# A gated linear attention feeding four experts: the state of two heads kept in 96 columns, their last features side by side

## The chip, the cores and the metric

The kernel runs on one core of a Trainium2 chip. The metric is the device time of one execution in microseconds (us). Engines are named as in the profile: PE is TensorE's matmuls and PEld its weight loads, DVE is VectorE, ACT is ScalarE, POOL is GpSimd, and SP is the queue that issues most DMAs.

## The reference: what is computed

```python
# q, k, v, alpha: (4 batches, 8 heads, 768 steps, 48 features)
for t in range(S):
    state = alpha[:, :, t, :, None] * state + einsum('bhd,bhe->bhde', k[:, :, t], v[:, :, t])
    y[:, :, t] = einsum('bhd,bhde->bhe', q[:, :, t], state)
x = y.transpose(0, 2, 1, 3).reshape(3072, 384)          # rows: batch and step; columns: head, feature
p = domain_probs / (domain_probs.sum(-1, keepdims=True) + 1e-9)
for e in range(4):                                        # w1: 384 x 1024, w2: 1024 x 384
    h = maximum(x @ w1[e], 0)
    out += p[:, e:e + 1] * (h @ w2[e])
```

Everything is float32. Each head carries a 48 x 48 state through 768 steps. The result of the eight heads, 384 columns, goes through four two-layer experts whose outputs are mixed by `p`.

## The kernel before

**Units.** The 768 steps are cut into 6 blocks of 128 (`cb`), and a unit is one block of one batch, all 8 heads: 24 units, in `attention(u)`. Heads are taken in pairs. A pair has 128 rows: 64 for each head, of which 48 hold features and 16 are zero. Within a unit, the scores between the 128 steps are built in seven levels (`copy_q`, `next_q`, `next_k`, `products`, `take`), and end in `lat`, a 128 x 128 matrix for each head. `QT` holds the decayed queries of the pairs, turned so that features are rows. `KT` holds the decayed keys.

**What a unit does with values and state.** `rv` holds v for the unit, 128 steps by 8 heads by 64 columns (`values`, two buffers). For the even head of a pair the 48 features lie in columns 0 to 47, with zeros behind. For the odd head the first 32 features lie in columns 0 to 31 and the last 16 (`TAIL`) in columns 48 to 63, with zeros between. `load` therefore moves v in three DMAs (L166 to L168) on SP's queue, one for the even heads and two for the odd ones. `sts[b]` is the state of batch b: 128 rows (features of the key, both heads of the pair) by 4 pairs by 2 heads by 64 columns (features of the value, laid out as in `rv`). Rows of one head against columns of the other stay zero, as they were set at the start.

**The read-out, L405 to L420.** `yps` receives the result turned, features in rows: 384 rows as 3 chunks of 128, each made of four strips of 32 rows. A turn is four matmuls, one for each strip. Each has 32 weight columns and 128 moving columns. Chunks 0 and 1 hold the first 32 features of the heads, one head to a strip. Chunk 2 holds the last 16 features of all heads, and a strip holds those of one pair: 16 of the even head, 16 of the odd head. Its strip is summed over two turns, one for each head, where the zeros beside each head's tail keep the other head's rows unchanged. A turn over the past multiplies the state with `QT`. A turn over the unit's own steps multiplies `rv` with `lat`. Units of the first block (`cb == 0`, 4 of the 24) have no past.

**The state update, L430 to L446,** is done for all blocks but the last: the keys are turned on PE and copied by ACT to `KB`; four matmuls, one for each pair, write keys with values into `sps` (L437, 128 weight columns, 128 moving columns). Then DVE, for each head of the pair, copies the sum into the state (block 0, L443) or multiplies the state with the decay of the block (L445) and adds the new sum (L446).

**Order of the work.** Nothing here is reordered by a scheduler: the program runs under a manual schedule, and each engine takes its instructions in the order in which the Python code emits them. The experts run in groups of up to four units. `up` makes hidden activations (L488, L496), `down` the outputs (L572, L576), `add_up` adds them to the accumulators on DVE (L603). `attention` is a generator with 17 beats, and `deal` gives each beat a due time from fixed estimates in `cost`. `advance`, called inside `up` and `down`, runs those beats that have come due. So the attention of the next units is dealt out between the experts' matmuls. In most groups the experts' products are made in three terms, and ACT and DVE prepare the parts between `up` and `down` (L503, L505, L528, L530, L538). At the start, matmuls on zeros (`fill`, L681, reading the last batch's state) keep PE running.

**DMAs.** Inputs, weights and most split weights come through SP's queue; `load(u + 2, "v")` is issued at the end of a unit for the unit two later. POOL clears `sts`, `values` and other tiles at the start (L659 to L667).

Of the kernel before, what the change touches and what calls it, by code (L numbers as in the profile page):

```python
# [10 lines left out]
F32 = mybir.dt.float32  # L11
# [9 lines left out]
def kernel(  # L21
# [37 lines left out]
    nc = tc.nc  # L59

    B, H, S, D = q.shape
    E, DM, F = moe_w1.shape
    P = 128
    NCB = S // P
    NP = H // 2
    HD = 64
    QUAD = 32
    TAIL = D - QUAD
# [13 lines left out]
    j = np.arange(P)[:, None] % HALF  # L82
    n = np.arange(QUAD)[None, :]
# [4 lines left out]
    const = ctx.enter_context(tc.tile_pool(name="const", bufs=1))  # L88
# [4 lines left out]
    ps = ctx.enter_context(tc.tile_pool(name="ps", bufs=2, space=bass.MemoryType.PSUM))  # L93
# [8 lines left out]

    near = const.tile([P, H, HALF], F32, name="near")
    lat = const.tile([P, H, P], F32, name="lat")
    sts = [const.tile([P, NP, 2, HD], F32, name=f"st{b}") for b in range(B)]

# [17 lines left out]
    def raw(u, nm):  # L126
        return values[u % 2] if nm == "v" else apart[nm] if u == 1 else early[nm]
# [26 lines left out]
    def load(u, names):  # L154
        if u >= len(units):
            return
        cb, b = units[u]
        for nm in names:
            src = srcs[nm][b, :, cb * P:(cb + 1) * P, :].rearrange("h s d -> s h d")
            if nm != "v":  # L160
                nc.sync.dma_start(out=raw(u, nm)[:, :, :D], in_=src)
                continue

            pairs = raw(u, nm).rearrange("p (a i) d -> p a i d", i=2)
            src = src.rearrange("p (a i) d -> p a i d", i=2)
            nc.sync.dma_start(out=pairs[:, :, 0, :D], in_=src[:, :, 0])  # L166
            nc.sync.dma_start(out=pairs[:, :, 1, :QUAD], in_=src[:, :, 1, :QUAD])
            nc.sync.dma_start(out=pairs[:, :, 1, D:], in_=src[:, :, 1, QUAD:])  # L168

# [86 lines left out]
    def turned(src):  # L258
        tp = ps.tile([P, NP, P], F32, name="tp", tag="w")
        for p in range(NP):  # L260
            nc.tensor.transpose(tp[:, p, :], src(p), ident)  # L261
        return tp

    def attention(u):
        cb, b = units[u]
        ra, rk, rq, rv = (raw(u, nm) for nm in ("a", "k", "q", "v"))
# [5 lines left out]
        nc.scalar.copy(out=AT, in_=turned(pair(ra)))  # L272
        after = u + 2 if u == 0 else u + 1 if u > 1 else len(units)
        load(after, "a")
        yield
        KT = keys()
# [3 lines left out]
        nc.vector.tensor_mul(own, rq[:, :, :D], rk[:, :, :D])  # L280
        nc.vector.reduce_sum(out=dot, in_=own, axis=AX.X)
        load(after, "k")
        yield
        nc.vector.tensor_mul(QT, turned(pair(rq)), AT)  # L284
        load(after, "q")
        yield

        decs = [AT]  # L290
# [91 lines left out]
        for r in range(NP // 2):  # L382
            for s in range(2):
                nc.tensor.matmul(far[HALF * s:HALF * (s + 1), r],
                                 lhsT=KTs[6][:, 2 * r + s, :HALF], rhs=qbs[6][:, 2 * r + s],
                                 start=True, stop=True)
# [8 lines left out]
        for s in range(2):  # L395
            rows = slice(HALF * s, HALF * (s + 1))
            nc.scalar.copy(out=parts[:HALF, :, s, :, HALF:], in_=far[rows])
        yield
        for s in range(2):
            rows = slice(HALF * s, HALF * (s + 1))  # L400
# [2 lines left out]
        yield  # L403

        st = sts[b]  # L405
        yps = ps.tile([P, KC, P], F32, name="yps", tag="w")
        for c in range(KC):

            if c < 2:
                turns = [[(j, 2 * c + j // 2, j % 2, slice(0, QUAD)) for j in range(4)]]  # L410
            else:
                turns = [[(p, p, i, slice(QUAD, HD)) for p in range(NP)] for i in range(2)]
            terms = [(t, past) for past in ((True, False) if cb > 0 else (False,)) for t in turns]
            for n, (turn, past) in enumerate(terms):
                for j, p, i, cols in turn:
                    nc.tensor.matmul(  # L416
                        yps[QUAD * j:QUAD * (j + 1), c, :],
                        lhsT=st[:, p, i, cols] if past else rv[:, 2 * p + i, cols],
                        rhs=QT[:, p, :] if past else lat[:, 2 * p + i, :],
                        start=(n == 0), stop=(n == len(terms) - 1))  # L420
        gi, slot = place[cb, b]
        if slot == 0:
            if gi == 0:
# [7 lines left out]
        if cb < NCB - 1:  # L431
            KB = AT
            nc.scalar.copy(out=KB, in_=turned(lambda p: KT[:, p, :]))
            yield
            sps = ps.tile([P, NP, 2, HD], F32, name="sps", tag="w")
            for p in range(NP):
                nc.tensor.matmul(sps[:, p], lhsT=KB[:, p, :], rhs=rv[:, 2 * p:2 * p + 2, :],  # L437
                                 start=True, stop=True)
            for i in range(2):
                rows = slice(HD * i, HD * (i + 1))  # L440
                old, add = st[rows, :, i, :], sps[rows, :, i, :]
                if cb == 0:
                    nc.vector.tensor_copy(out=old, in_=add)  # L443
                else:
                    nc.vector.tensor_mul(old, old, decs[-1][rows].broadcast_to([HD, NP, HD]))  # L445
                    nc.vector.tensor_add(old, old, add)  # L446

        load(u + 2, "v")
# [170 lines left out]
    def deal():  # L619

        wanted = [0.0]
        ends = [0.0, 0.0]
        events = []
        t = 0.0
        for gi in range(len(groups)):
            for e in range(E):
                part = 1 - 1 / len(groups[0]) if gi == e == 0 else 1
                t += cost(0, gi, e) * FCH * part  # L630
                if e == E - 1:
                    wanted.append(t)
                t += cost(1, gi, e) * len(groups[gi]) * part
        for gi in range(1, len(groups)):
            n = len(groups[gi])
            first = wanted[gi - 1] if gi > 1 else 0.0
            space = (wanted[gi] - MARGIN - first) / (n if gi > 1 else (n + 1) / 2)
            if gi == 1:
                space /= 2
            for k in range(n):  # L640
                u = sum(map(len, groups[:gi])) + k
                end = wanted[gi] - MARGIN - (n - 1 - k) * space
                begin = max(end - 2 * space, ends[-2])
                ends.append(end)
                run = attention(u)
                events += [(begin + (end - begin) * (j + 1) / BEATS, u, run) for j in range(BEATS)]
        return sorted(events, key=lambda x: x[:2])
# [7 lines left out]
    with tc.manual_schedule():  # L655
# [23 lines left out]
        def fill(n):  # L679
            for _ in range(n):  # L680
                nc.tensor.matmul(idle, lhsT=zeros, rhs=zeros, start=True, stop=True)  # L681

        runs = [attention(u) for u in range(len(groups[0]))]
        fill(8)
        for u, n in ((0, 3), (0, 6), (0, 4), (0, 5), (0, 5), (0, 4), (0, 3), (1, 0), (0, 0), (0, 2),
# [18 lines left out]
        for gi, e in ((gi, e) for gi in range(len(groups)) for e in range(E)):  # L704
# [5 lines left out]
            turns = [range(k, k + each) for k in range(rest, len(groups[gi]), each)]  # L710
# [41 lines left out]
```

## Time and profile before

| | |
|---|---|
| median of 7 runs | 1103.61 us (1103.15 to 1103.99) |
| the profiled execution | 1103.98 us, of which its span is 1102.2 us |
| busy in the span | PE 97%, PEld 82%, DVE 68%, ACT 51%, POOL 3% |
| granted TensorE clock, mean | 0.992 of full speed |
| DMA | 273.68 MB, mean 248 GB/s |
| matmul records | 8532; two for each plain float32 matmul |

A line of the group view gives the source line, the engine, the operation, the tiles written and read, the shape, the number of instructions, then the busy time of the group, the mean duration of one in ns, and the idle time of the engine before them with what ended it. Durations of matmuls overlap, since they are pipelined: a record of 275 ns can be followed by the next after 110 ns. The chain of waits is the chain of work that ended last: it is followed back from the end through whatever released each step.

### The profile page before, as it was taken

The numbers are of one execution on the slowest core, as the hardware profiler recorded it, in microseconds if no ns is written. First come the engines' busy times: TensorE is split into PE (matmuls) and PEld (weight loads), VectorE is DVE, ScalarE is ACT, GpSimd is POOL, SyncE is SP. The second block draws the span as 40 slices with busy tenths as digits, with TensorE's granted clock in tenths as the row PEclk, the third lists the DMA queues.
The fourth block names the chain that finished last, engine by engine and source line by source line (L and its number), as shares of the span: only waits on it lengthen the run. The fifth ranks groups of instructions, "written<-read, shape, count | busy, mean of one in ns | idle before, by whom it ended". The sixth has DMA issues, their size and how long they took to land.

```text
span 1102.2 us, 21700 instructions
## 1 busy us (share of the span) xinstructions
PE 1069.2 (97%) x8532; PEld 898.3 (82%) x8532; DVE 752.1 (68%) x1625; ACT 562.1 (51%) x1191; POOL 35.4 (3%) x75
## 2 busy tenths in 40 slices
PE   8889899999999999998999999899999999999998
PEld 8767677676776889897898898798888898898876
DVE  5577777656558868768778778787786776657211
ACT  5786776575556554544545535455444354323321
POOL 2000000000000000000000000000000000000000
PEclk9999999999999999999999999899999999999999
DMA  8597689877696965955758658477478468545882
GB/s 122 157 321 237 198 288 376 289 272 274 206 317 215 405 235 176 349 199 198 304 168 296 263 148 328 154 262 305 161 274 305 155 271 341 216 199 247 297 318 87
DMA packets 166197, 273.68 MB, mean 248 GB/s; under 512 B 120624, under 2 KB 140976, under 8 KB 142032
## 3 DMA queue, kind: packets, MB, share of 16 engines
q1 hardware_dynamic: 156704, 230.06, 59.8%
q0 software_dynamic: 6016, 42.08, 9.6%
q8 instruction: 67, 1.10, 0.4%
q10 hardware_dynamic: 3376, 0.17, 0.3%
q14 instruction: 34, 0.28, 0.1%
HBM read 229.81 MB, written 42.47 MB: 247 GB/s over the span
## 4 chain that ended last, share of the span: by engine, by line
PE 76%; DVE 14%; ACT 7%; issue 3%; DMA 1%; SPq 0%; ACTq 0%; DVEq 0%
PE ops L572 19%; PE one L496 17%; PE ops L576 14%; PE two L496 8%; PE sc L329 5%; PE yps L416 4%; PE one L488 3%; DVE hT L530 3%; DVE t L505 2%; DVE hT L538 2%; PE tp L261 2%; ACT qb L303 2%; ACT hT L528 2%; DVE near L339 2%; PE sps L437 1%
## 5 line engine op out<-in xcount | busy, mean ns | idle before, releaser
L572 PE MATMUL ops<-w,hT 128*128 128x384 f32 x1536 | 290.8, 344 | 12.1 <-DVE acc L603 11.9
L572 PEld LDWEIGHTS ops<-w,hT 128*128 128x128 f32 x1536 | 269.9, 190 | 17.4 <-DVE acc L603 14.5
L496 PE MATMUL one<-xT,w 128*128 128x512 f32 (+1 forms) x1104 | 274.8, 385 | 0.9 <-DVE hT L508 0.8
L496 PEld LDWEIGHTS one<-xT,w 128*128 128x128 f32 x1104 | 194.9, 188 | 42.6 <-issue 3.2
L503 ACT ACTIVATE t<-one 128x512 f32<-128x512 f32 (+1 forms) x184 | 103.2, 561 | 159.2 <-PE one L496 158.7
L303 ACT COPY qb<-QT 64x256 f32<-64x256 f32 x336 | 136.5, 406 | 81.4 <-DVE QT L284 48.0
L576 PE MATMUL ops<-hT 128*128 128x384 f32 x512 | 176.3, 492 | 0.0
L496 PE MATMUL two<-xT,w 128*128 128x512 f32 (+1 forms) x552 | 148.4, 377 | 0.0
L576 PEld LDWEIGHTS ops<-hT 128*128 128x128 f32 x512 | 94.0, 191 | 56.0 <-issue 0.8
L528 ACT ACTIVATE hT<-t 128x512 fp32r<-128x512 f32 x128 | 80.9, 632 | 97.3 <-DVE t L505 96.2
L530 DVE SCALAR_TENSOR_TENSOR hT<-t,hT 128x512 fp32r<-128x512 f32 x128 | 88.7, 693 | 61.1 <-ACT hT L528 59.7
L496 PEld LDWEIGHTS two<-xT,w 128*128 128x128 f32 x552 | 100.4, 188 | 19.7
L603 DVE SCALAR_TENSOR_TENSOR acc<-ops,p_all,acc 128x384 f32<-128x384 f32 x88 | 54.2, 617 | 75.2 <-PE ops L576 43.5
L538 DVE SCALAR_TENSOR_TENSOR hT<-hT 128x256 fp32r<-128x256 f32 x256 | 100.9, 422 | 4.4
L505 DVE TENSOR_TENSOR t<-t,two 128x512 f32<-128x512 f32 x128 | 87.4, 683 | 20.7 <-PE two L496 12.4
L339 DVE COPY_PREDICATED near<-masks,sc 128x256 f32<-128x256 uint8 x144 | 77.1, 535 | 21.7 <-PE sc L329 18.7
L329 PEld LDWEIGHTS sc<-qb,KT 128*64 128x64 f32 x2304 | 73.9, 140 | 9.6 <-issue 7.6
L329 PE MATMUL sc<-qb,KT 128*64 128x64 f32 x2304 | 78.2, 225 | 0.3 <-ACT qb L303 0.3
L508 DVE TENSOR_TENSOR hT<-t,two 128x512 f32<-128x512 f32 (+1 forms) x56 | 32.1, 574 | 67.2 <-ACT t L503 58.1
L310 DVE TENSOR_TENSOR QT<-QT,dec 128x256 f32<-128x256 f32 x144 | 60.8, 422 | 24.9 <-ACT qb L303 24.3
L322 DVE TENSOR_TENSOR KT<-KT,dec 128x256 f32<-128x256 f32 x144 | 60.4, 419 | 1.7 <-PE tp L261 1.5
L321 ACT COPY KT<-KT 128x256 f32<-128x256 f32 x144 | 59.8, 415 | 3.1
(79 smaller groups left out, 929.4 us busy)
## 6 DMA issues: line engine op xcount, KB each, us to landing
w<-kept SPq DMA_DIRECT2D x156, 1152.0 KB
kept<-w POOLq DMA_DIRECT2D x32, 1152.0 KB, 7.5
hT<-in_moe_w_dram SPq DMA_DIRECT2D x48, 384.0 KB
w<-in_moe_w_dram SPq DMA_DIRECT2D x60, 128.0 KB
ra<-in_alpha_dram SPq DMA_DIRECT2D x23, 192.0 KB
rk<-in_k_dram SPq DMA_DIRECT2D x23, 192.0 KB
rq<-in_q_dram SPq DMA_DIRECT2D x23, 192.0 KB
out_dram<-acc POOLq DMA_DIRECT2D x22, 192.0 KB, 6.6
```

Source lines behind the costliest of these rows:

```text
L303: nc.scalar.copy(out=qb[rows, :, i, :].rearrange("p a (b r) -> p a b r", r=m), in_=qv[rows])
L310: nc.vector.tensor_mul(qv, qv, spread(dv[:, :, :, 0], m))
L329: nc.tensor.matmul(out[HALF * s:HALF * (s + 1), 2 * p:2 * p + 2, :], lhsT=KTs[li][:, p, HALF * s:HALF * (s + 1)], rhs=qbs[li][:, p, :, QUA ...
L339: nc.vector.copy_predicated(near.rearrange("p a (b two r) -> p a b two r", two=2, r=m)[:, :, :, 1, :], mk.unsqueeze(1).broadcast_to([P, H, ...
L496: nc.tensor.matmul(out, lhsT=w[:, part, kc], rhs=xTs[gi][:, part, kc, :n], start=(part == terms[0] and kc == 0), stop=(part == terms[-1] a ...
L503: nc.scalar.activation(out=t, in_=one, func=ACT.Copy, scale=FINE)
L505: nc.vector.tensor_add(t, t, two)
L528: nc.scalar.activation(out=top, in_=x, func=ACT.Relu, scale=TRIM)
L530: nc.vector.scalar_tensor_tensor(out=low, in0=x, scalar=0.0, in1=top.bitcast(F32), op0=ALU.max, op1=ALU.subtract)
L538: nc.vector.scalar_tensor_tensor(out=dif, in0=top.bitcast(F32), scalar=1 / 4096.0, in1=low.bitcast(F32), op0=ALU.mult, op1=ALU.subtract)
L572: nc.tensor.matmul(sums[i][part // 2], lhsT=h[:, part], rhs=w, start=(fc == 0 and part != 1), stop=(fc == FCH - 1 and part != 0))
L576: nc.tensor.matmul(sums[i][0], lhsT=h[:, 2].bitcast(F32), rhs=w, start=(fc == 0), stop=(fc == FCH - 1))
```

## The change

State and keys-with-values are 48 columns a head in place of 64, so 96 for a pair. For the odd head the last 16 features now come first, followed by the first 32: in the 96 columns of a pair the two heads' tails stand side by side, in columns 32 to 63. In `rv` the head's 64 columns stay, with the odd head's tail in columns 0 to 15 and its first 32 features in columns 16 to 47. For the past, chunk 2 is read from the state in one turn, since one slice of 32 columns holds both tails and rows of one head are zero against the other's columns. For the unit's own steps chunk 2 is still read in two turns, with the zeros of `rv` beside each tail.

```diff
-    sts = [const.tile([P, NP, 2, HD], F32, name=f"st{b}") for b in range(B)]
+    sts = [const.tile([P, NP, 2, D], F32, name=f"st{b}") for b in range(B)]
...
-            nc.sync.dma_start(out=pairs[:, :, 1, :QUAD], in_=src[:, :, 1, :QUAD])
-            nc.sync.dma_start(out=pairs[:, :, 1, D:], in_=src[:, :, 1, QUAD:])
+            nc.sync.dma_start(out=pairs[:, :, 1, :TAIL], in_=src[:, :, 1, QUAD:])
+            nc.sync.dma_start(out=pairs[:, :, 1, TAIL:D], in_=src[:, :, 1, :QUAD])
...
         st = sts[b]
+        flat_st = st.rearrange("p a i d -> p a (i d)")
+        flat_v = rv.rearrange("p (a i) d -> p a (i d)", i=2)
         yps = ps.tile([P, KC, P], F32, name="yps", tag="w")
         for c in range(KC):
             if c < 2:
-                turns = [[(j, 2 * c + j // 2, j % 2, slice(0, QUAD)) for j in range(4)]]
+                now = [[(2 * c + j // 2, j % 2, (0, HD + TAIL)[j % 2], 2 * QUAD * (j % 2))
+                        for j in range(4)]]
+                turns = ([(True, now[0])] if cb > 0 else []) + [(False, now[0])]
             else:
-                turns = [[(p, p, i, slice(QUAD, HD)) for p in range(NP)] for i in range(2)]
-            terms = [(t, past) for past in ((True, False) if cb > 0 else (False,)) for t in turns]
-            for n, (turn, past) in enumerate(terms):
-                for j, p, i, cols in turn:
+                turns = [(True, [(p, 0, 0, QUAD) for p in range(NP)])] if cb > 0 else []
+                turns += [(False, [(p, i, QUAD + TAIL * i, 0) for p in range(NP)]) for i in range(2)]
+            for n, (past, turn) in enumerate(turns):
+                for j, (p, i, in_v, in_st) in enumerate(turn):
                     nc.tensor.matmul(
                         yps[QUAD * j:QUAD * (j + 1), c, :],
-                        lhsT=st[:, p, i, cols] if past else rv[:, 2 * p + i, cols],
+                        lhsT=flat_st[:, p, in_st:in_st + QUAD] if past
+                        else flat_v[:, p, in_v:in_v + QUAD],
                         rhs=QT[:, p, :] if past else lat[:, 2 * p + i, :],
-                        start=(n == 0), stop=(n == len(terms) - 1))
+                        start=(n == 0), stop=(n == len(turns) - 1))
...
-            sps = ps.tile([P, NP, 2, HD], F32, name="sps", tag="w")
+            sps = ps.tile([P, NP, 2, D], F32, name="sps", tag="w")
             for p in range(NP):
-                nc.tensor.matmul(sps[:, p], lhsT=KB[:, p, :], rhs=rv[:, 2 * p:2 * p + 2, :],
+                nc.tensor.matmul(sps[:, p], lhsT=KB[:, p, :], rhs=rv[:, 2 * p:2 * p + 2, :D],
                                  start=True, stop=True)
...
-                    nc.vector.tensor_mul(old, old, decs[-1][rows].broadcast_to([HD, NP, HD]))
+                    nc.vector.tensor_mul(old, old, decs[-1][rows].broadcast_to([HD, NP, D]))
```

## The prediction

> **What bounds the kernel now.** I read busy time by engine first, then the chain of waits, then the list of who waited for whom (us in total, times, longest).
>
> ```profile
> PE 1069.2 (97%) x8532; PEld 898.3 (82%) x8532; DVE 752.1 (68%) x1625; ACT 562.1 (51%) x1191; POOL 35.4 (3%) x75
> PE 76%; DVE 14%; ACT 7%; issue 3%; DMA 1%; SPq 0%; ACTq 0%; DVEq 0%
> ```
>
> ```profile
> PE ops L572 <- DVE acc L603: 11.9, 7, 3.8
> ```
>
> PE is the bound: it is idle for 33 us in all, and three quarters of the chain lie on it. The last line is its longest wait, for DVE's accumulation, where experts and attention together have filled DVE. PE waits for no DMA in that list. So a PE instruction saved counts if the chain runs through its burst, and DVE work counts only where the chain runs on DVE. The chain in order of time (start, length, work) tells which:
>
> ```profile
> 488.20 1.93 PE yps L416 x64
> ...
> 490.15 0.03 ACT x_raw L428
> ...
> 501.68 0.34 DVE st L445
> ...
> 518.63 0.54 DVE acc L603
> ...
> 519.22 4.67 PE ops L572 x17
> ...
> 1027.98 2.59 PE one L488 x12
> 1030.58 10.32 PE ops L576 x32
> ```
>
> The read-out's burst stands on the chain in all 20 units that have a past, from 124.98 to 980.69 us. After the one shown the chain goes through ACT to DVE, over the state update, to the accumulation that PE waits for. It crosses a whole state update so four times, at 501, 593, 676 and 769 us. It crosses the burst of sps in 15 of 20 units. The last two lines serve as a ruler: plain float32 matmuls follow each other every 0.216 us with 256 moving columns (2.59 / 12) and every 0.3225 us with 384 (10.32 / 32). Durations come from the groups with shapes kept apart (busy us, mean ns of one, idle before), and from the timeline (start, length from first start to last end):
>
> ```profile
> L416 PEld LDWEIGHTS yps<-QT,st 128*32 128x32 f32 x640 | 17.1, 109 | 7.3 <-issue 6.5 <-ACT hT L528 0.7
> L437 PEld LDWEIGHTS sps<-rv,AT 128*128 128x128 f32 x160 | 20.7, 191 | 3.9 <-ACT AT L433 1.8
> L329 PEld LDWEIGHTS sc<-qb,KT 128*64 128x64 f32 x2304 | 73.9, 140 | 9.6 <-issue 7.6 <-PE tp L261 1.1 <-ACT qb L303 0.8
> L446 DVE TENSOR_TENSOR st<-st,sps 64x256 f32<-64x256 f32 x32 | 13.4, 419 | 6.9 <-PE sps L437 5.0
> L312 DVE TENSOR_TENSOR dec<-AT 128x256 f32<-128x256 f32 x24 | 10.1, 419 | 0.0
> L312 DVE TENSOR_TENSOR dec<-dec 128x128 f32<-128x128 f32 x24 | 6.8, 285 | 0.0
> ```
>
> ```profile
> 489.03 0.62 PE L416 MATMUL yps<-QT,st 128*32 128x128 f32 x16
> 489.47 0.62 PE L416 MATMUL yps<-lat,rv 128*32 128x128 f32 x16
> 498.83 1.05 PE L437 MATMUL sps<-rv,AT 128*128 128x128 f32 x8
> ```
>
> **The change part by part.** The lists of instructions of the two kernels, engine by engine, are the same in order but for what follows.
>
> *The turn removed.* In chunk 2 the past takes one turn in place of two: 4 matmuls, 8 records, less in each of 20 units. Two turns over the past, 16 records, start at 489.03 and the next two at 489.47, so a turn takes 0.22 us: its four strips run beside each other, and its two records a strip follow each other after 109 ns. All 20 bursts are on the chain: 20 x 0.219 = 4.4 us. Its price is known; what could hide it is a second path nearly as long, which is a rival below. Waits of the burst for `lat` (7.7 us, 5 times) come at or before the other turns and stay.
>
> *Keys with values in 96 columns.* Four matmuls, 8 records, in 20 units, with the same 128 weight columns and 96 moving columns in place of 128. The records now follow each other after (1.05 - 0.276) / 7 = 0.111 us, 0.276 being the mean length of one in its group. No row has 96 columns, so I bound it. If the stream of columns set the pace, the ruler's (0.3225 - 0.216) / 128 = 0.83 ns a column gives 0.216 - 160 x 0.00083 = 0.083 us, which saves 8 x 0.028 = 0.22 us a burst, 3.4 us over the 15 on the chain. If the weight load sets it, nothing is saved, or as far as the load reaches down. A load of 32, 64 and 128 columns takes 109, 140 and 191 ns, so 0.8 ns a column lies above a fixed part: 128 columns need some 105 ns. In this burst each load starts together with the matmul before it (starts of the trace, 2 ns apart), so the next matmul can't come sooner than that. Between the ends, 0.083 and 0.111, I take 0.108, by the loads: 0.003 x 8 x 15 = 0.4 us. A loss is not excluded by a row for two runs of 48 columns in place of one of 128, but the matmuls of sc already stream two runs of 32 and keep their pace.
>
> The Trainium skill, "TensorE: Matmul & The Clock Gate", section "LDWEIGHTS (loading the stationary operand)", states that a load takes its number of columns over 1.2 in ns, whatever the rows, which makes 107 ns here. It speaks against this half of the change: by it the saving is 4 ns a record, 0.5 us over the 15 bursts, where the ruler alone would give 3.4 us. No run here shows yet a matmul of 96 columns behind 128 columns of weights.
>
> *State update on DVE.* 8 copies and 64 multiplies and adds over 192 elements in place of 256. Rows of 256 and 128 elements take 419 and 285 ns, 1.05 ns an element, and the row on 64 partitions agrees with that on 128; so 352 ns, 67 ns less each, 4.8 us of DVE's time. Four updates, of 4 instructions, are on the chain: 16 x 0.067 = 1.1 us. The first unit's copy at 35.45 us adds 0.1. The other 3.6 us lie beside a running PE; were DVE the bound there too, they would add to the gain, so this cover is no risk.
>
> *v's DMAs.* The same three transfers, bytes and pieces; the odd heads' 64-byte pieces now go ahead of their 128-byte pieces, on SP's queue, with the same transfers behind. v of unit u + 2 is asked for at 499.91 us and first read at 581.7, so 80 us cover it. Without that cover the swap could cost the time by which one of the two transfers lands later than the other, and PE waits for no landing of v in the list; I take 0.
>
> *Clearing the state.* Four memsets on POOL over 384 elements in place of 512: the rows of 512 and 128 take 524 and 204 ns, so 0.1 us less each. The first lets the matmuls on zeros start 0.1 us sooner, but the chain then runs on the landing of q at 8.96 us, so 0; at most 0.1 us gained.
>
> Sum: 4.4 + 0.4 + 1.1 + 0.1 = 6.0 us. The profiled execution took 1103.98 us (span 1102.2), which is 0.37 us above the median shown: 1098.0 by its own time, 1097.6 by the median. I forecast 1097.8.
>
> **The rivals.**
> - *The stream sets the pace of sps:* 3.0 us more is saved: 1094.8. For it: 0.111 is also near the ruler's 0.109 for 128 columns, so the row alone does not tell load from stream. Against: the loads' lengths and starts above.
> - *Another path takes over.* The shortened chain is the least that the time can become; another path may then be the longest, and where the chain leaves PE right after the burst, ACT and DVE may hardly have been waiting for it. For it: 21% of the chain is on DVE and ACT. Against: at 490.15 ACT had waited 1.63 us for the burst, and DVE's next work on QT 1.59 us, much more than 0.22. If ten turns and the four updates came to nothing, 2.2 + 1.1 us are lost: 1101.1. If nearly all did, the time would be within 0.2% (2.2 us, about what a measurement of this kernel can tell from no change).
> - *Slower: weights from `rv` off their old boundaries.* The odd head's slices now start 192 and 320 bytes into a pair's row; all weights of yps so far start at multiples of 128 bytes. No row shows such a load. Of the 8 groups of four records over `rv` in each of 24 units, 192 in all, each would have to lose 31 ns to eat the 6.0 us. Doubling a group's 109 ns would cost 21 us: 1119. Against: the slices are still whole runs of 32 elements, and no row of the profile shows a load that is longer for where it starts.
>
> **How the numbers follow.** My forecast, 4.4 to 7 us saved: 0.66. The stream: 0.11. Another path taking part of the gain: 0.17, of which half stays beyond 0.2%. Slower: 0.04, and 0.02 for no change otherwise. Faster is 0.66 + 0.11 + 0.09 = 0.86, same 0.10, slower 0.04. The range goes down to the stream's end, 1094.5, and up to the absorbed case, 1101.3.
>
> **What would show it.** In the changed profile: 480 records of yps from the state in place of 640, and a burst with a past of 56 records, 0.22 us shorter. The sps burst of 8 at 1.0 us or a little more (0.86 if the stream sets it). DVE's L445 and L446 at about 352 ns, DVE's busy time 4.8 us lower. The chain still on all 20 bursts, and PE's wait for L603 near 11 to 12 us. Wrong would be: yps groups over `rv` more than 109 ns apart, a longer wait of yps for `lat` or of L572 for L603, or a PE wait for v's DMAs.

## The result, and the profile after

The changed kernel takes 1096.89 us (median of 15 executions, 1093.75 to 1099.69) against 1103.61 us before. The ratio is 0.9941, 95% interval 0.9932 to 0.9949: 6.7 us faster (5.6 to 7.5). The forecast was 1097.8 us, 5.8 us faster. The profiled execution took 1093.75 us with a span of 1092.0 us. It is the quickest of the 15, so its span is not to be held against the 1102.2 us of before without more: 10 us lie between the two, and about half of that is not the change, as the section on the granted clock shows.

Busy time by engine and chain of waits of the changed kernel, from its page:

```profile
PE 1060.1 (97%) x8372; PEld 889.2 (81%) x8372; DVE 747.2 (68%) x1625; ACT 561.4 (51%) x1191; POOL 35.0 (3%) x75
PE 74%; DVE 13%; ACT 7%; issue 3%; DMA 2%; SPq 0%; ACTq 0%; DVEq 0%
```

160 records have gone from PE and 4.9 us of busy time from DVE. PE is still the bound. Who PE waited for (us in total, times, longest):

```profile
PE ops L579 <- DVE acc L610: 10.8, 7, 3.5
PE yps L422 <- ACT lat L402: 7.7, 5, 3.5
PE one L503 <- DMA w<-kept: 1.4, 2, 0.7
```

The wait for DVE's accumulation fell from 11.9 to 10.8 us, the wait for `lat` stayed as it was, and a wait for split weights is in the list that was not there. Groups with shapes kept apart (busy us, mean ns of one, idle before):

```profile
L422 PE MATMUL yps<-QT,st 128*32 128x128 f32 x480 | 24.6, 277 | 0.0
L444 PE MATMUL sps<-rv,AT 128*128 128x96 f32 x160 | 20.8, 273 | 1.3 <-ACT AT L440 1.3
L453 DVE TENSOR_TENSOR st<-st,sps 64x192 f32<-64x192 f32 x32 | 11.3, 352 | 7.1 <-PE sps L444 5.2
```

DVE's update takes 352 ns an instruction, as worked out from the rows of 128 and 256 elements. The read-out and the sums in the timeline (start, length from first start to last end), in the unit that was shown of before:

```profile
486.91 0.40 PE L422 MATMUL yps<-QT,st 128*32 128x128 f32 x8
487.13 0.62 PE L422 MATMUL yps<-lat,rv 128*32 128x128 f32 x16
...
496.49 1.02 PE L444 MATMUL sps<-rv,AT 128*128 128x96 f32 x8
```

Chunk 2 has one turn over the past, 0.22 us, where it had two. Turns over `rv` are still 0.22 us apart. The sums' burst went from 1.05 to 1.02 us only.

**The granted clock.** Executions of one kernel on one chip differ by up to 6 us, and they differ in step with the mean TensorE clock that they were granted: 12 executions of before with 0.992 took 1103.5 us in the mean, 20 with 0.995 took 1100.6 us. The traces show stretches of 3.4 us in which the clock is halved, most of them at one of PE's longer waits. In such a stretch, at 519.7 us of before, the matmuls of `ops` follow each other after 0.32 us; at the same place of the changed kernel, at full clock, it is 0.17 us. Windows of 40 us around the two longest waits for DVE (busy us of each engine, PE's clock, DMA share, GB/s), before:

```profile
500.00:540.00 40.00, 36.24 (x280) 32.68 (x282) 32.90 (x72) 18.26 (x40) 2.16 (x4) 0.96 0.54 185
680.00:720.00 40.00, 36.37 (x286) 33.10 (x282) 31.14 (x69) 19.01 (x41) 2.16 (x4) 0.91 0.50 179
```

and the changed kernel:

```profile
500.00:540.00 40.00, 36.49 (x324) 32.69 (x323) 33.61 (x75) 19.43 (x43) 2.16 (x4) 1.00 0.60 208
680.00:720.00 40.00, 36.51 (x312) 32.21 (x311) 32.89 (x73) 20.85 (x45) 2.16 (x4) 0.96 0.59 221
```

One stretch in 40 us makes 0.96, two make 0.91. The profiled execution of before has five of them in the work of the kernel, that of the changed kernel two. But a second profile of the changed kernel, below, has six, so the number is a matter of the execution. To compare kernels I fitted straight lines to the 142 executions in the table, time against granted clock, with a height of its own for each set and one slope for all: 0.83 us for 0.001 of clock. (For the 35 executions of before in the first comparison no clock of each is on record, so they are not among them.) One stretch of 3.4 us at half clock is 0.0016 of the mean clock in 1100 us, so about 1.3 us. The times "at equal clock" below are the heights at 0.993, with standard errors of 0.1 to 0.3 us:

| kernel | executions | median us | mean clock | at equal clock |
|---|---|---|---|---|
| before | 57 | 1102.4 | 0.9934 | 1102.6 |
| before, for a second look | 10 | 1102.9 | 0.9925 | 1102.7 |
| changed (two sets) | 15 and 9 | 1096.9 and 1098.7 | 0.9935 and 0.9918 | 1097.3 and 1097.2 |
| two turns over the past | 12 | 1101.9 | 0.9931 | 1101.8 |
| DVE's time given back | 12 | 1099.7 | 0.9924 | 1098.8 |
| multiply on POOL (two sets) | 6 and 5 | 1092.8 and 1092.8 | 0.9945 and 0.9954 | 1094.5 and 1094.4 |
| low part of x on POOL too | 12 | 1103.7 | 0.9896 | 1101.1 |
| multiply and near on POOL | 4 | 1091.1 | 0.9960 | 1093.6 |

At equal clock the change is worth 5.3 us. The 24 executions of the changed kernel had a mean clock of 0.9928, no higher than before's 0.9934, so this leaves out nothing of what the change brought. For the kernels with the multiply on POOL, whose clock is higher, the last column leaves out what the clock adds.

### The profile page after: what moved, and what is told of

Read it like the earlier page. It is cut to its first block, busy times and chain, and to the rows that moved or that the text cites. A ratio compares the mean times of both kernels' runs of the same rounds, so it can differ in the third digit from the quotient of the medians.

```text
span 1092.0 us, 21380 instructions
## 1 busy us (share of the span) xinstructions
PE 1060.1 (97%) x8372; PEld 889.2 (81%) x8372; DVE 747.2 (68%) x1625; ACT 561.4 (51%) x1191; POOL 35.0 (3%) x75
## 4 chain that ended last, share of the span: by engine, by line
PE 74%; DVE 13%; ACT 7%; issue 3%; DMA 2%; SPq 0%; ACTq 0%; DVEq 0%
PE ops L579 20%; PE one L503 18%; PE ops L583 13%; PE two L503 8%; PE sc L330 5%; PE yps L422 3%; PE one L495 3%; DVE hT L537 3%; DVE t L512 2%; PE tp L262 2%; ACT qb L304 2%; DVE hT L545 2%; ACT hT L535 2%; DVE near L340 1%; PE far L385 1%
## 5 line engine op out<-in xcount | busy, mean ns | idle before, releaser
L579 PE MATMUL ops<-w,hT 128*128 128x384 f32 x1536 | 287.7, 342 | 10.9 <-DVE acc L610 10.8
```

What stands on the lines that cost most here:

```text
L579: nc.tensor.matmul(sums[i][part // 2], lhsT=h[:, part], rhs=w, start=(fc == 0 and part != 1), stop=(fc == FCH - 1 and part != 0))
```

## The experiments

Three theories stood against each other. Theory 1 is the prediction's: the gain is the sum of the steps, each by what of it lies on the chain. Theory 2: a good part of the measured gain is the clock. Theory 3: the gain is DVE's 4.8 us less work, and the turn is hidden.

### The changed kernel again

> The changed kernel itself, beside the kernel before on the same chip. Theory 1 (the gain is the sum of the steps: the turn 4.4 us, the update on DVE 1.1, the shorter sps 0.5): 6.0 us faster, ratio 0.9946, and executions whose granted clock is equal differ by 6.0 us. Theory 2 (a good part of the gain are stretches in which TensorE runs at half clock, fewer by luck in some executions): the spans of single executions follow the mean granted clock, 0.001 of clock being worth about 1 us, and at equal clock less than 5 us are left.

Measured: 1098.71 us against 1102.25 us, ratio 0.9966 (0.9952 to 0.9979), so 3.7 us faster where the first comparison had 6.7. The mean clock of these 9 executions is 0.9918 against 0.9934 before. At equal clock 5.3 us remain, and the two sets of the changed kernel agree within 0.2 us. Theory 2 is right on the spread of the medians and wrong on the rest: about 5 us are the change itself.

### The past read in two turns

```diff
-    sts = [const.tile([P, NP, 2, D], F32, name=f"st{b}") for b in range(B)]
+    sts = [const.tile([P, NP, 2, HD], F32, name=f"st{b}") for b in range(B)]
...
-                now = [[(2 * c + j // 2, j % 2, (0, HD + TAIL)[j % 2], 2 * QUAD * (j % 2))
+                now = [[(2 * c + j // 2, j % 2, (0, HD + TAIL)[j % 2], (0, HD + TAIL)[j % 2])
...
-                turns = [(True, [(p, 0, 0, QUAD) for p in range(NP)])] if cb > 0 else []
+                turns = [(True, [(p, i, 0, QUAD + TAIL * i) for p in range(NP)]) for i in range(2)] if cb > 0 else []
...
-                old, add = st[rows, :, i, :], sps[rows, :, i, :]
+                old, add = st[rows, :, i, :D], sps[rows, :, i, :]
```

> The state is 64 columns a head again, laid out like v, and the past of chunk 2 is read in two turns; the sums stay 96 columns wide and DVE's updates 192 elements. Theory 1 (the turn counts in full): 4.4 us slower than the changed kernel, about 1101.3, 1.6 faster than the kernel before; bursts with a past have 64 records and last 0.22 us longer. Theory 3 (the gain is DVE's 4.8 us less work, the turn is hidden): at most 1 us slower than the changed kernel, about 1097.5.

Measured: 1101.94 us, ratio to before 0.9996 (0.9985 to 1.0007). At equal clock it is 4.5 us slower than the changed kernel and 0.8 us faster than before. Its read-out, chunk 2:

```profile
488.37 0.62 PE L422 MATMUL yps<-QT,st 128*32 128x128 f32 x16
488.81 0.62 PE L422 MATMUL yps<-lat,rv 128*32 128x128 f32 x16
```

The turn is worth 4.5 us, what 20 turns of 0.22 us sum to. Theory 3 falls. All else in the change, the sums and DVE together, is worth 0.8 us and not the 1.6 forecast. Each of the two is good to about 0.2 us.

### The time given back to DVE

```diff
+            if cb > 0:
+                nc.vector.tensor_mul(pad[:, :112], ident[:, :112], ident[:, :112])
```

> The changed kernel with one more DVE instruction after each update of a state with a past, which writes a tile that nobody reads and takes about 0.27 us, the time by which the four instructions of the update became shorter: 16 x 0.27 = 4.3 us of DVE's time. Theory 1 (only the four updates on the chain count): 1.1 us slower than the changed kernel, about 1098.0. Theory 3 (DVE's work counts everywhere): 4.3 us slower, about 1101.2. If DVE's work is hidden everywhere: equal.

Measured: 1099.71 us, ratio to before 0.9972 (0.9961 to 0.9983); at equal clock 1.5 us slower than the changed kernel. The instruction takes 275 ns, 4.4 us in all. PE's waits:

```profile
PE ops L582 <- DVE acc L613: 11.8, 7, 4.0
...
PE one L498 <- DMA w<-in_moe_w_dram: 0.8, 1, 0.8
```

The wait for the accumulation is back from 10.8 to 11.8 us. So a quarter of the 4.4 us of DVE's time counts, where the chain crosses the update, and the rest is hidden. Of the 1.5 us that leaves 0.5, about twice the errors of the two heights. The second line is a wait, near 1020 us, that is in neither profile of the changed kernel and may be this rest; whether the other executions have it is not shown.

### Sums with 48 moving columns, and with 64 weight columns

```diff
-                nc.tensor.matmul(sps[:, p], lhsT=KB[:, p, :], rhs=rv[:, 2 * p:2 * p + 2, :D],
+                nc.tensor.matmul(sps[:, p, 0], lhsT=KB[:, p, :], rhs=rv[:, 2 * p, :D],
...
-                old, add = st[rows, :, i, :], sps[rows, :, i, :]
+                old, add = st[rows, :, i, :], sps[rows, :, 0, :]
```

> The matmuls of sps move 48 columns, the even head's values alone, behind the same 128 columns of weights; both heads of a pair get the even head's sum, so the odd head's state is left out. If the weight load sets the pace: records follow each other after 0.105 to 0.108 us as with 96 columns, the burst from first to last start stays 0.75 us. If the stream of columns sets it: 0.04 to 0.06 us apart, the burst about 0.35 us.

```diff
-                nc.tensor.matmul(sps[:, p], lhsT=KB[:, p, :], rhs=rv[:, 2 * p:2 * p + 2, :D],
+                nc.tensor.matmul(sps[:HD, p], lhsT=KB[:, p, :HD], rhs=rv[:, 2 * p:2 * p + 2, :D],
...
-                old, add = st[rows, :, i, :], sps[rows, :, i, :]
+                old, add = st[rows, :, i, :], sps[:HD, :, i, :]
```

> The matmuls of sps have 64 weight columns in place of 128, the even head's keys alone, and move 96 columns as in the changed kernel; both heads' states get the even head's sum, so the odd head's state is left out. The weight load of 64 columns takes 0.14 us, of which some 0.053 depends on the columns. If the load set the pace at 0.111 us with 128 columns, now the stream of 96 columns sets it: records 0.083 us apart, 0.58 us from first to last start. If something else holds a record at 0.111 us, the burst stays at 0.75 us.

Each of the two ran once (1097.87 and 1100.08 us), so it is their traces that are read. The burst in the timeline, first 48 columns behind 128 weight columns:

```profile
498.91 0.98 PE L444 MATMUL sps<-rv,AT 128*128 128x48 f32 x8
```

and 96 columns behind 64 weight columns:

```profile
498.77 0.88 PE L444 MATMUL sps<-rv,AT 128*64 128x96 f32 x8
```

With 128 weight columns the burst takes 1.05 us for 128 moving columns, 1.02 for 96 and 0.98 for 48. In the records of the trace the starts lie 0.111 us apart in all three, but for the first gap of the burst, which is 0.109, 0.082 and 0.042 us (medians of 20 bursts): the second load comes with the first matmul, and from then on the loads set the pace. With 64 weight columns the records follow each other after 0.083 us, but for a first gap of 0.133 us; that is the stream of 96 columns as the ruler gave it. So with 128 weight columns the load sets the pace of the sums, and the rival by which the stream does is refuted. Fewer weight columns would bring no gain here for all that: the first of these matmuls starts 0.085 us later behind the work ahead of it than in the changed kernel, and the fourth matmul behind the burst 0.09 us later. Why was not tried.

The traces say more. I aligned the matmuls of the kernel before and of the changed kernel one by one and took by how much the distance between the two grows from the last matmul ahead of a burst of sums to the fourth behind it. It grows by 0.0 us over all 20 bursts together. The 0.03 us that a burst is shorter are gone by the second matmul behind it; the loads of a burst lie 0.90 us apart from the first to the last in both kernels.

### The second profile of before

The kernel is the one before, unchanged.

> The kernel before, for a second look. In four profiles of kernels with the shorter state PE waits 0.7 to 1.5 us for split weights near 170 us, in the one profile of before it doesn't. If this wait comes of the change (PE now reaches these weights sooner): none here, 0.2 us at most. If it differs from one execution to the next: 0.5 us or more here too.

Measured: 1102.85 us, ratio 1.0002 (0.9987 to 1.0017). Its waits for weights:

```profile
PE one L496 <- DMA w<-kept: 0.8, 1, 0.8
```

So the wait as such is not new: in the first profile of before the same matmul waited 0.85 us as well, put down there to DVE. New is a second one just ahead of it. The changed kernel's timeline where the first split weights are used (idle before and releaser in brackets):

```profile
170.47 1.62 PE L503 MATMUL one<-xT,w 128*128 128x512 f32 x6 [0.67 <-DMA w<-kept]
...
175.96 1.62 PE L503 MATMUL one<-xT,w 128*128 128x512 f32 x6 [0.68 <-DMA w<-kept]
```

and that of before:

```profile
170.92 1.64 PE L496 MATMUL one<-xT,w 128*128 128x512 f32 x6
...
176.60 1.62 PE L496 MATMUL one<-xT,w 128*128 128x512 f32 x6 [0.85 <-DVE hT L508]
```

In both profiles of the changed kernel, and in those with time given back to DVE or work on POOL, PE is idle at both places (0.5 to 0.8 us each). In two profiles of before, and with two turns over the past, it waits once (0.8 to 1.0 us). With the matmuls of the first profiles of the two kernels aligned, PE is done with the work ahead of these weights 1.05 us sooner than before. Two turns are 0.44 us of that; the rest comes mostly from the start and from shorter waits for ACT. Behind both places it is 0.64 us ahead: 0.4 us are taken back, and by the waits it is 0.5.

The first of these weights are asked for 1.05 us sooner too, at 160.09 in place of 161.14 us, but land only 0.44 us sooner, at 170.34 in place of 170.78: the transfer took 10.25 us where it had taken 9.64. In before too the first matmul starts just behind the landing, by 0.14 us, but PE had been idle for 0.07 us only. Why the transfer was longer was not tried. It took 9.1 to 9.6 us in the two profiles of before and with two turns, 10.3 to 10.7 us in those of the changed kernel and with time given back to DVE, and 9.2 us again in three of the four with the multiply on POOL, so one turn less does not settle its length.

### Work moved from DVE to POOL

The four places where the chain crosses the update ask for more than 64 columns less. POOL is idle.

```diff
-                    nc.vector.tensor_mul(old, old, decs[-1][rows].broadcast_to([HD, NP, D]))
+                    eng = nc.gpsimd if gi > 2 else nc.vector
+                    eng.tensor_mul(old, old, decs[-1][rows].broadcast_to([HD, NP, D]))
```

> From the fourth group of units on (10 of the 20 updates, the four on the chain among them) the state is multiplied with its decay by POOL in place of DVE, which takes 2 x 0.352 us from DVE in each. Theory 1 (DVE's work counts where the chain crosses the update, four times, by what lies in PE's waits for the accumulation): these waits fall by 4 x 0.70 = 2.8 us, from 10.8 to about 8, and at equal clock the kernel is about 2.8 us faster than the changed one. If POOL's multiply is later than the sums or slows DVE beside it: equal or slower. Theory 2 (TensorE falls to half clock after its long waits): with the longest waits near 2.8 us instead of 3.5, fewer such stretches and a higher granted clock, a further 1 to 3 us.

Measured: 1092.80 us, ratio to before 0.9915 (0.9899 to 0.9932). Waits and POOL's group:

```profile
PE ops L580 <- DVE acc L611: 8.2, 5, 2.6
```

```profile
L453 POOL TENSOR_TENSOR st<-st,dec 64x192 f32<-64x192 f32 x20 | 11.0, 548 | 299.4 <-PE yps L422 219.2 <-DVE t L513 40.6 <-DVE hT L546 38.8
```

PE's waits fall by 2.6 us and the time at equal clock by 2.8 us. No wait for POOL's multiply is in the list, though it takes 548 ns where DVE took 352; but six of DVE's instructions beside it take 0.2 to 0.3 us longer than elsewhere. This confirms where DVE's work counts: behind the four updates on the chain PE's waits fall by 2.4 us, everywhere else by 0.3. The sum of four times 0.70 us came out partly by luck: the two long waits, near 517 and 689 us, fall from 3.5 to 2.6 us each, by more than 0.70, and the two short ones, near 601 and 775 us, had only 0.3 us each to lose. The mean clock is 0.9945, and 0.9952 over the 15 executions of this kernel, its repeat and the last one below, against 0.9934 before: half-clock stretches are fewer. Run again for its interval:

> The kernel with the multiply on POOL again, for its interval: 1092 to 1095 us by theory 1 and 2, ratio to the kernel before 0.990 to 0.993, mean granted clock above that of the kernel before.

Measured: 1092.79 us, ratio 0.9918 (0.9903 to 0.9934), mean clock 0.9954.

The low part of x on POOL in addition:

```diff
-        nc.vector.tensor_sub(low, x, top.bitcast(F32))
+        (eng or nc.vector).tensor_sub(low, x, top.bitcast(F32))
...
-            split(xraws[gi][:, kc, :n], [xTs[gi][:, part, kc, :n] for part in range(3)])
+            split(xraws[gi][:, kc, :n], [xTs[gi][:, part, kc, :n] for part in range(3)],
+                  nc.gpsimd if gi > 2 else None)
```

> In addition to the multiply, POOL makes the low part of x (three instructions of 0.69 us a group on DVE, four groups from the fourth on). Theory 1: where these lie on the chain ahead of the accumulation, PE's waits for it fall by up to 0.7 us more in each group, to 5 to 6 us in all, and the kernel is up to 2 us faster than with the multiply alone. If POOL takes over 1.5 us for each, the expert's next products wait for it: slower.

Measured: 1103.67 us, ratio 1.0011 (1.0001 to 1.0021): the whole gain is lost, 6.7 us at equal clock against the multiply alone.

```profile
PE ops L581 <- DVE acc L612: 14.9, 5, 4.4
```

```profile
L244 POOL TENSOR_TENSOR xT<-x_raw,xT 128x512 fp32r<-128x512 f32 x9 | 13.1, 1459 | 149.1 <-ACT xT L243 107.0 <-PE ops L581 42.1
```

POOL takes 1459 ns where DVE takes 686, but DVE waits for its result only once, 1.2 us. What grows are DVE's own instructions beside POOL's. DVE's timeline ahead of the wait near 517 us, with the multiply alone:

```profile
511.11 0.17 DVE L313 TENSOR_TENSOR dec<-dec 128x16 f32<-128x16 f32 x1
...
514.33 0.75 DVE L546 SCALAR_TENSOR_TENSOR hT<-hT 128x256 fp32r<-128x256 f32 x2
```

and with the low part of x on POOL too, then POOL's own:

```profile
511.85 1.26 DVE L313 TENSOR_TENSOR dec<-dec 128x16 f32<-128x16 f32 x1
...
515.44 1.82 DVE L547 SCALAR_TENSOR_TENSOR hT<-hT 128x256 fp32r<-128x256 f32 x2
```

```profile
511.64 1.44 POOL L244 TENSOR_TENSOR xT<-x_raw,xT 128x512 fp32r<-128x512 f32 x1 [21.07 <-PE ops L581]
515.54 1.44 POOL L244 TENSOR_TENSOR xT<-x_raw,xT 128x512 fp32r<-128x512 f32 x1 [2.46 <-ACT xT L243]
```

Neither line of DVE reads or writes x, and yet both are longer, by 1.09 and 1.07 us, and end 0.03 and 0.28 us after POOL's. DVE saves 0.68 us here by the one instruction that it no longer makes, so it comes 1.5 us later to the accumulation, and PE's wait grows from 2.64 to 4.08 us. In the whole kernel eleven of DVE's instructions beside POOL's are 0.4 to 1.1 us longer than elsewhere. So the waits of PE grow, where the forecast had them shrink, and not because of POOL's late result, which was the loss it named. What holds DVE was not tried, and not all of its instructions are held: the accumulation, 0.62 us, started and ended within one of POOL's. Moving work off a full engine does not help if the other engine's work makes the full engine's own instructions longer.

The filling of `near` on POOL in place of the low part of x:

```diff
-        nc.vector.tensor_mul(near, ident_all[:, P:].unsqueeze(1).broadcast_to([P, H, HALF]),
+        (nc.gpsimd if place[cb, b][0] > 2 else nc.vector).tensor_mul(near, ident_all[:, P:].unsqueeze(1).broadcast_to([P, H, HALF]),
```

> The kernel with the state's multiply on POOL, and from the fourth group on POOL also fills near (128 x 512 elements, 0.69 us on DVE). Theory 1: this instruction lies on the chain right behind the update in the four stretches, so PE's waits for the accumulation fall by up to 4 x 0.69 = 2.8 us, from 8.2 to 5.5, and at equal clock the kernel is 2 to 2.8 us faster than with the multiply alone. If POOL's 1.46 us for such a shape are late for the first scores: no gain, as with the low part of x. Theory 2: the longest wait falls from 2.6 to about 1.9 us, fewer stretches at half clock, mean granted clock at or above 0.995.

Measured: 1091.07 us, ratio to before 0.9908 (0.9894 to 0.9921), 0.8 us faster at equal clock than the multiply alone, not 2 to 2.8.

```profile
PE ops L580 <- DVE acc L611: 7.2, 5, 2.4
```

The waits fall by 1.0 us in place of 2.8. `near` stood on the chain, but with it gone the chain there runs through the experts' hidden parts, from DVE to ACT and back, and at the two longest waits only 0.2 us came of it. Here too eleven of DVE's instructions beside POOL's filling, 1.05 us each, are 0.2 to 0.8 us longer than elsewhere. This is the fastest version measured, 11 us faster than the kernel before by the medians and 9 us at equal clock.

## Why the prediction was right or wrong

**The turn removed: right.** 0.22 us less in each of 20 bursts, all on the chain, in the changed kernel's too, and 480 records in place of 640. Undone by itself it costs 4.5 us; the term was 4.4.

**Keys with values: mis-sized.** The term was 0.4 us, from taking 0.108 us between records. They stay 0.111 us apart, only the first gap is shorter, and the work behind begins when it did: 0.0 us. That the load sets the pace was right, and carrying it to its end would have given this: the pace that I had measured, 0.111, was the load's already. The 105 ns that I took for the load rest on 0.8 ns a column, which is the step from 64 to 128 columns; from 32 to 128 columns the same rows give (191 - 109) / 96 = 0.85 ns a column, 109 ns. The section "LDWEIGHTS (loading the stationary operand)" of the Trainium skill's page "TensorE: Matmul & The Clock Gate" gives a load as its columns over 1.2 in ns, by which I estimate 107 ns for this one. The runs agree that the load and not the stream bounds the burst, and show 0.111 us from record to record. The 4 ns a record in between were not to be had.

**The update on DVE: right in place, and nearly in size.** 352 ns an instruction; the wait for the accumulation fell by 1.1 us, and rose by 1.0 when the time was given back. It did not fall by 0.27 us at each of the four places, but by 0.1 to 0.4.

**What the sum left out:** the split weights near 170 us, which take back 0.4 to 0.5 us. The prediction had read that PE waits for no DMA, and asked of v's transfers alone what could become late next. The list showed no wait because PE was idle for only 0.07 us before the first of these weights had landed, and it doesn't tell how near a longer wait was.

So 4.5 for the turn and 0.8 for the rest is 5.3 us, against a sum of 6.0. The 0.7 that lack are about the 0.4 of the sums and the 0.4 to 0.5 at the split weights; the two experiments' numbers, good to 0.2 us each, don't show that loss apart. The measured median, 6.7 us below that of before, lies on the other side of the sum. I put that down to the clock of those executions, but for before's it is not on record, so this is not shown. That 1096.89 lies so near the forecast of 1097.8 us is partly luck: the second set of the same kernel had 1098.71, only 3.7 us below before. v's DMAs cost nothing, as no wait for v is in any list, and POOL's clearing is 0.1 us shorter, as worked out (524 to 418 ns). Turns over `rv` with slices off the old boundaries still run at 0.22 us, so the slower rival falls too. Another path did take over, but for 0.4 to 0.5 us.

## What to carry to other kernels

Price a removed PE instruction by the pace in its burst, not by the mean of one, and check by the chain in order of time that each burst stands on it. A matmul with fewer moving columns gains nothing if the load of its weights sets the pace: compare the distance between records with the load's length for fewer weight columns before the stream is made shorter. Where the chain crosses another engine just ahead of PE's longest waits, a fraction of that engine's work, here four updates of twenty, was worth about all of its time, as far as the waits had that much to lose. An idle engine can take it if nothing in the old queue waits for its result, and if the old engine's instructions beside it do not become longer: compare their lengths with and without.

## What the runs showed of the hardware

Stretches of 3.4 us at half the TensorE clock go with some 5 of the 6 us between executions of one and the same program here (0.989 to 0.995 of clock at 0.83 us for 0.001), as much as the change itself. In all twelve profiles one begins near 81 us, at a wait of PE of 2.7 us. Others lie near 124, 517 and 692 us, at waits of 2.4 to 4.1 us, sometimes two in a row, and near 864 us, in both profiles of before at a wait of 1.9 us. They do not come in every execution: before's first profile has none at its wait of 3.5 us near 125 us. With the waits for DVE at 2.4 to 2.7 us the one near 692 us was absent from three profiles, and one of 3.4 us near 517 was still there. So no length of wait comes out of these traces above which a stretch follows. The medians of 15 and of 9 executions of the changed kernel differed by 1.8 us; held against the granted clock, which is listed for each execution, the two sets agree within 0.2 us.

An instruction of DVE that starts while POOL works on a tensor can be held until POOL's ends: one on 128 x 16 elements took 1.26 us in place of 0.17 and ended 0.03 us after POOL's.
